# Two groups of set-up work placed later in a transformer block written in float32: row statistics of eight input tiles, and the loads for the next weight fold

## The chip, the cores and the metric

The kernel runs on one core of a Trainium2 chip. The metric is device time in microseconds (us). Three runs of the kernel before gave a median of 1911.75 us (1910.15 to 1915.11).

## The reference, cut to what matters

One block of a transformer on x of 2048 rows by 1024 columns, all float32:

```python
qkv = layernorm(x) @ wqkv                      # 32 heads of 32
pq, pk = q @ w_phi, k @ w_phi                  # per head
phi = concat(softmax(p), softmax(-p))          # for pq and for pk
o = (phi_q @ (phi_k.T @ v)) / (phi_q @ sum(phi_k) + 1e-6)
h = x + o @ wo
out = h + relu(layernorm(h) @ w1) @ w2
```

The layer norm divides by the square root of variance plus 1e-5 and has no learned scale.

## The kernel before, in words

**Tiles.** x is cut into 16 row tiles of 128 rows (t = 0 to 15). Products are float32 made of three matmuls each: every operand is split into a high part and a low part, and `mm3` (lines 181 to 184) adds high by high, high by low and low by high in PSUM. The second of the three, line 183, is the first that reads the low part of a weight.

**Items and steps.** The work of TensorE is a list of items, and each item has steps. In the stage of this change an item is one row tile times a set s of 512 weight columns: eight steps k = 0 to 7, one for each 128 rows of the weight, each step three matmuls. Items 0 to 31 (steps 0 to 255) are the keys and values of x tiles 0 to 7: eight items for each s = 0 to 3, so that s = 1 starts at step 64, s = 2 at step 128 and s = 3 at step 192. Items 32 to 47 (from step 256) are the queries of the same tiles, then the keys, values and queries of x tiles 8 to 15 follow.

**An order written out by hand.** Nothing is scheduled by a compiler. `when(step, f, ...)` puts a call beside a step, and the program walks through the steps in order and lets each call issue its instructions. Each engine, and the queue of SP that starts almost all DMAs, then works through its own instructions strictly in that order. An instruction that waits holds all that stand behind it on its engine. A step number says only where in these queues an instruction stands, not when it runs. Inside one step the calls run in the order in which they were registered in the code.

**What stands around the change in the queues.**

- Weight units. For each (s, k) SP loads a 128 by 512 tile `raw` (lines 324 and 325, or 328 for queries; six buffers), ScalarE copies the high part into `w` (line 125), and VectorE (odd units) or GpSimd (even units) subtracts to get the low part (line 129). There are ten buffers for `w`. Eight hold the present s, so the units k = 0 and 1 of the next s are made ahead, and each later one only when the last item of the present s has used up a unit.
- Folds. w_phi is multiplied into the weights of keys and queries once. Fold p (p = 1 to 7) stands at the steps `FOLD_STEPS` = 31, 64, 104, 144, 176, 206, 232. There TensorE multiplies two loaded tiles `wt` (`fold_all`, line 290) and VectorE transposes the result (`fold_turn`, line 300). Six steps later SP stores 1 MB to DRAM (`fold_store`, line 311), and 17 steps later the raw loads that read it may be issued. `wt_load` (line 274) issues the two loads of 512 KB for the next fold; it has four buffers.
- Sums of w1 and w2. From step 24 on, every ten steps, number n: `t_load` at step 24 + 10n (`b`, 512 KB, line 351), four subtractions in place on GpSimd at 31 to 34 + 10n (`t_sum`, line 361), `t_store` at 37 + 10n (line 364). `b` has two buffers, so load n waits on the SP queue until store n - 2 has landed.
- Statistics of x tiles 8 to 15. These tiles are loaded twice. The first time, with key ("s", t), only the two numbers of the layer norm are taken: `ln_load` at step `early` = 80 + 16 (t - 8) (`xin`, 512 KB, two buffers, line 215), `ln_stats` on VectorE at `early` + 10 (two statistics instructions of line 221 and one of line 223, result `mv`), `ln_power` on GpSimd at `early` + 13 (lines 230 to 232, three instructions on one column, result `scx`). The second load, from step 241 on, reads the rows again and normalizes them with `scx`.
- Keys and values of an item n, after its matmuls: VectorE (lines 428 to 432), ScalarE exponential at 8n + 11 (line 436), VectorE at 8n + 13 (lines 441 to 444, result `kphi`), GpSimd's running sum `zacc` at 8n + 18 (line 452), and small matmuls that read `kphi` (line 463).

Of the kernel before, what the change touches and what calls it, by code (L numbers as in the profile page):

```python
# [140 lines left out]
def kernel(  # L141
# [12 lines left out]
    v, act, pool, pe, sp = nc.vector, nc.scalar, nc.gpsimd, nc.tensor, nc.sync  # L154
# [34 lines left out]
    def do(n, k, f, *args):  # L189
        at[n, k].append((f, args))  # L190
# [17 lines left out]
    xin, xst, xnt = {}, {}, {}  # L208
# [644 lines left out]
    def item(gen, *args, keys):  # L853
        items.append((gen, args + (keys,)))
        steps.extend((k,) for k in keys)
        return len(items) - 1
# [11 lines left out]
    for b, tiles in enumerate(groups):  # L868
        for hf in range(2):

            pairs = b == 0 and hf == 0
            for j in range(0, 4, 2 if pairs else 1):
# [3 lines left out]
                for half in range(2):  # L876
                    n = item(wo_pair, tiles[j:j + 2], hf, half, keys=[("wo", hf, 4 * half + k // 2) for k in range(8)])
# [18 lines left out]
    def x_part(t):  # L896
        return [x[t * P:(t + 1) * P, :]]
# [6 lines left out]
    def when(step, f, *args):  # L904

        if step < 8 * first_up:
            do(step // 8, step % 8, f, *args)
        else:
            do(first_up + (step - 8 * first_up) // 4, step % 4, f, *args)
# [4 lines left out]
    for t in range(1, NT):  # L914
        n = t - 1 if t < HT else q_n[1, t - HT] + 1
        turn = 8 * n + 1
        if t < HT:
            stages = X_STEPS.get(t, (turn - 22, turn - 12, turn - 9, turn - 6, turn, turn + 3))
        else:

            early = 80 + 16 * (t - HT)
            when(early, ln_load, ("s", t), x_part(t))
            when(early + 10, ln_stats, ("s", t))
            when(early + 10, xin.pop, ("s", t))
            when(early + 13, ln_power, ("s", t))
            load_ = turn - 88 + 8 * (t - HT) if t < HT + 4 else turn - 36
            stages = (load_, None, None, turn - 8, turn, turn + 3)
        for step, f, *args in zip(stages, (ln_load, ln_stats, ln_power, ln_norm), [("x", t)] * 4):
            if step is not None:
                when(step, f, *args, *([x_part(t)] if f is ln_load else []))  # L930
        do(n, 0, x_open, t)
        for j in range(2):
            when(stages[4 + j], ln_turn, ("x", t), j, lambda t=t: xT[t])
# [6 lines left out]
    for p, n in enumerate(FOLD_STEPS, 1):  # L940
        when(n, fold_all, p)
        when(n, fold_turn, p)
        when(n + 6, fold_store, p)
        when(n + 17, fold_ready, p)
        if p < 7:
            when(n + 2, wt_load, p + 1, sp)


    for (hf, s, t), n in kv_n.items():
# [146 lines left out]
    for b in range(2):  # L1096
        for m in DOWN:
            n = down_n[b, m, NP - 1] + 1
# [112 lines left out]
```

## Time and profile before

| | |
|---|---|
| median of three runs | 1911.75 us |
| profiled execution, its own time | 1911.77 us |
| its span, first to last instruction | 1910.0 us |
| TensorE busy with matmuls | 1884.6 us (99%) |
| VectorE, ScalarE, GpSimd busy | 1045.3, 739.2, 975.8 us |
| mean granted TensorE clock | 0.996 |
| mean DMA rate | 226 GB/s |

How to read it: the profile comes from one execution. Its time is 1.8 us over its span and agrees with the median of the runs. A stage is read from its own part of the trace: the times below are microseconds from the start of the span. In the timeline of an engine each row has the start, the duration, the engine (SPq is the queue of SP), the line, the instruction with what it writes and reads, how many are merged, and in brackets how long the engine sat idle before it and for whom. A wait for several things is put down to the one that came last.

### The profile page before, as it was taken

The numbers are of one execution on the slowest core, as the hardware profiler recorded it, in microseconds if no ns is written. First come the engines' busy times: TensorE is split into PE (matmuls) and PEld (weight loads), VectorE is DVE, ScalarE is ACT, GpSimd is POOL, SyncE is SP. The second block draws the span as 40 slices with busy tenths as digits, with TensorE's granted clock in tenths as the row PEclk, the third lists the DMA queues.
The fourth block names the chain that finished last, engine by engine and source line by source line (L and its number), as shares of the span: only waits on it lengthen the run. The fifth ranks groups of instructions, "written<-read, shape, count | busy, mean of one in ns | idle before, by whom it ended". The sixth has DMA issues, their size and how long they took to land.

```text
span 1910.0 us, 31857 instructions
## 1 busy us (share of the span) xinstructions
PE 1884.6 (99%) x11640; PEld 1540.9 (81%) x11640; DVE 1045.3 (55%) x1685; ACT 739.2 (39%) x1258; POOL 975.8 (51%) x961
## 2 busy tenths in 40 slices
PE   9979999999999999999999999999999999999999
PEld 7757778877878888888888888888888888888887
DVE  7858668767669866545644564344433333343333
ACT  5322225322222212345454464444444444444442
POOL 4667751789955988523333232222244444444443
PEclk9989999999999999999999999999999999999999
DMA  6879785666666667696777897566677677877775
GB/s 213 264 232 303 250 268 189 220 189 210 206 192 204 210 207 242 216 302 219 254 257 231 262 290 235 178 189 194 213 243 225 191 240 225 250 214 218 216 215 178
DMA packets 292366, 432.17 MB, mean 226 GB/s; under 512 B 24049, under 2 KB 150001, under 8 KB 292209
## 3 DMA queue, kind: packets, MB, share of 16 engines
q1 hardware_dynamic: 275312, 413.36, 68.5%
q10 hardware_dynamic: 16896, 16.78, 2.6%
q8 instruction: 91, 1.49, 0.3%
q14 instruction: 67, 0.54, 0.1%
HBM read 292.68 MB, written 137.36 MB: 225 GB/s over the span
## 4 chain that ended last, share of the span: by engine, by line
PE 83%; POOL 7%; DMA 6%; issue 1%; DVE 1%; SPq 0%; ACT 0%; POOLq 0%; DVEq 0%; ACTq 0%
PE mm L182 21%; PE mm L183 21%; PE mm L184 21%; PE ac L183 4%; PE ac L184 4%; PE ac L182 4%; POOL b L361 3%; DMA b<-in_w_dram 3%; PE tp L183 2%; PE tp L184 2%; PE tp L182 2%; POOL w L129 2%; DMA t<-b 2%; DMA xin<-in_x_dram 1%; PE tp L245 1%
## 5 line engine op out<-in xcount | busy, mean ns | idle before, releaser
L129 POOL TENSOR_TENSOR w<-raw,w 128x512 fp32r<-128x512 f32 x355 | 474.7, 1339 | 717.7 <-ACT w L125 665.0
L125 ACT ACTIVATE w<-raw 128x512 fp32r<-128x512 f32 x686 | 408.7, 626 | 507.8 <-PE mm L184 246.6
L129 DVE TENSOR_TENSOR w<-raw,w 128x512 fp32r<-128x512 f32 x331 | 270.5, 818 | 529.1 <-ACT w L125 525.8
L183 PE MATMUL mm<-w,xT 128*128 128x512 f32 x768 | 302.8, 394 | 14.7 <-POOL w L129 14.2
L182 PE MATMUL mm<-w,xT 128*128 128x512 f32 x768 | 309.3, 403 | 0.0
L184 PE MATMUL mm<-w,xT 128*128 128x512 f32 x768 | 301.2, 392 | 0.0
L182 PE MATMUL mm<-hT,w 128*128 128x512 f32 x672 | 262.7, 391 | 0.0
L183 PE MATMUL mm<-hT,w 128*128 128x512 f32 x672 | 261.6, 389 | 0.6 <-DVE hT L753 0.6
L184 PE MATMUL mm<-hT,w 128*128 128x512 f32 x672 | 261.6, 389 | 0.0
L361 POOL TENSOR_TENSOR b<-b 128x256 f32<-128x256 f32 x224 | 181.5, 810 | 99.2 <-DMA b<-in_w_dram 84.5
L183 PEld LDWEIGHTS mm<-w,xT 128*128 128x128 f32 x768 | 145.3, 189 | 48.9 <-POOL w L129 19.1
L182 PEld LDWEIGHTS mm<-w,xT 128*128 128x128 f32 x768 | 145.2, 189 | 35.1 <-issue 4.2
L184 PEld LDWEIGHTS mm<-w,xT 128*128 128x128 f32 x768 | 145.2, 189 | 30.7
L182 PE MATMUL mm<-w 128*128 128x512 f32 x392 | 152.5, 389 | 0.0
L183 PE MATMUL mm<-w 128*128 128x512 f32 x392 | 152.5, 389 | 0.0
L184 PE MATMUL mm<-w 128*128 128x512 f32 x392 | 152.5, 389 | 0.0
L183 PEld LDWEIGHTS mm<-hT,w 128*128 128x128 f32 x672 | 126.2, 188 | 26.8 <-DVE hT L753 1.1
L184 PEld LDWEIGHTS mm<-hT,w 128*128 128x128 f32 x672 | 126.1, 188 | 26.4
L182 PEld LDWEIGHTS mm<-hT,w 128*128 128x128 f32 x672 | 126.1, 188 | 26.0 <-ACT c L776 0.3
L436 ACT ACTIVATE ke<-ke 128x512 f32<-128x512 f32 x64 | 40.4, 631 | 121.2 <-DVE ke L432 121.2
L182 PEld LDWEIGHTS mm<-w 128*128 128x128 f32 x392 | 73.6, 188 | 15.3
L183 PEld LDWEIGHTS mm<-w 128*128 128x128 f32 x392 | 73.6, 188 | 15.3
(169 smaller groups left out, 3135.1 us busy)
## 6 DMA issues: line engine op xcount, KB each, us to landing
raw<-t SPq DMA_DIRECT2D x224, 256.0 KB, 3.9
raw<-ad SPq DMA_DIRECT2D x196, 256.0 KB, 3.0
raw<-in_w_dram SPq DMA_DIRECT2D x168, 256.0 KB, 3.1
b<-in_w_dram SPq DMA_DIRECT2D x56, 512.0 KB, 3.9
t<-b SPq DMA_DIRECT2D x56, 512.0 KB, 4.7
ad<-c SPq DMA_DIRECT2D x112, 256.0 KB, 3.5
ad<-s SPq DMA_DIRECT2D x84, 256.0 KB, 4.2
ed<-qe ACTq DMA_DIRECT2D x32, 512.0 KB, 4.4
```

Source lines behind the costliest of these rows:

```text
L125: nc.scalar.activation(w[:, 0, :], raw[1], AF.Copy)
L129: eng.tensor_tensor(out=w[:, 1, :], in0=raw[1], in1=w[:, 0, :].bitcast(F32), op=ALU.subtract)
L182: pe.matmul(ps, a_hi, b_hi, start=first, stop=False, skip_group_check=more)
L183: pe.matmul(ps, a_hi, b_lo, start=False, stop=False, skip_group_check=more)
L184: pe.matmul(ps, a_lo, b_hi, start=False, stop=last, skip_group_check=more)
L245: pe.transpose(pt[:, k, :], xn[:, (4 * j + k) * P:(4 * j + k + 1) * P], ident)
L361: pool.tensor_tensor(out=tsum[j, *out], in0=tsum[j, *a], in1=tsum[j, *b], op=ALU.subtract)
L436: act.activation(e_of[key], e_of[key], AF.Exp)
```

## The change

For x tiles 8 to 15, `ln_stats` goes from `early` + 10 to `early` + 18, and `ln_power` from `early` + 13 to `early` + 22. The loads `ln_load` stay at `early`. The bookkeeping call `xin.pop` goes along and issues nothing. Apart from that, `wt_load` for fold p + 1 goes from two steps behind fold p to twelve: from steps 33, 66, 106, 146, 178, 208 to 43, 76, 116, 156, 188, 218. No instruction is added or removed.

```diff
             early = 80 + 16 * (t - HT)
             when(early, ln_load, ("s", t), x_part(t))
-            when(early + 10, ln_stats, ("s", t))
-            when(early + 10, xin.pop, ("s", t))
-            when(early + 13, ln_power, ("s", t))
+            when(early + 18, ln_stats, ("s", t))
+            when(early + 18, xin.pop, ("s", t))
+            when(early + 22, ln_power, ("s", t))
...
         when(n + 6, fold_store, p)
         when(n + 17, fold_ready, p)
         if p < 7:
-            when(n + 2, wt_load, p + 1, sp)
+            when(n + 12, wt_load, p + 1, sp)
```

## The prediction

> **What bounds the kernel now.** I read the page first. TensorE is busy almost the whole span, so a change of order can win only what TensorE loses: idle time and time at a low clock.
>
> ```profile
> PE 1884.6 (99%) x11640; PEld 1540.9 (81%) x11640; DVE 1045.3 (55%) x1685; ACT 739.2 (39%) x1258; POOL 975.8 (51%) x961
> PEclk9989999999999999999999999999999999999999
> ```
>
> The only lowered clock digit is the third slice of 47.75 us (95 to 143 us), which is where the moved calls stand. The waits of TensorE from 100 to 140 us, and its timeline there:
>
> ```profile
> PE mm L183 <- POOL w L129: 9.6, 2, 8.4
> ```
>
> ```profile
> 118.78 0.43 PE L463 MATMUL ac<-kphi,vt 128*32 128x64 f32 x16 [0.67 <-DVE kphi L444]
> ...
> 122.91 0.50 PE L183 MATMUL mm<-w,xT 128*128 128x512 f32 x1 [1.21 <-POOL w L129]
> ...
> 132.93 0.80 PE L183 MATMUL mm<-w,xT 128*128 128x512 f32 x1 [8.37 <-POOL w L129]
> ...
> 138.40 0.43 PE L183 MATMUL mm<-w,xT 128*128 128x512 f32 x1
> 138.66 0.39 PE L184 MATMUL mm<-w,xT 128*128 128x512 f32 x1
> 138.89 0.39 PE L182 MATMUL mm<-w,xT 128*128 128x512 f32 x1
> ```
>
> TensorE stops where set s = 2 begins (step 128): at the low part of unit k = 2, and for 8.37 us at that of k = 4. Behind the stop the clock is low: from 132.93 to 138.40 stand 12 intervals, 5.47 us, which at the later pace of 0.23 us take 2.7. The whole place costs 0.67 + 1.21 + 8.37 + 2.74 = **13.0 us**. That is the ceiling of the gain here.
>
> Next question: why are the low parts late? GpSimd and VectorE around it:
>
> ```profile
> 101.11 0.22 POOL L230 TENSOR_SCALAR scx<-mv 128x1 f32<-128x1 f32 x1
> ...
> 102.30 1.57 POOL L361 TENSOR_TENSOR b<-b 128x256 f32<-128x256 f32 x2
> 103.83 1.29 POOL L129 TENSOR_TENSOR w<-raw,w 128x512 fp32r<-128x512 f32 x1
> ...
> 113.18 0.22 POOL L230 TENSOR_SCALAR scx<-mv 128x1 f32<-128x1 f32 x1 [2.41 <-DVE mv L223]
> ...
> 116.53 2.70 POOL L361 TENSOR_TENSOR b<-b 128x256 f32<-128x256 f32 x3 [1.68 <-DMA b<-in_w_dram]
> ...
> 121.60 1.26 POOL L129 TENSOR_TENSOR w<-raw,w 128x512 fp32r<-128x512 f32 x1
> 127.75 1.12 POOL L361 TENSOR_TENSOR b<-b 128x256 f32<-128x256 f32 x1 [4.89 <-DVE mv L223]
> ...
> 131.17 1.71 POOL L129 TENSOR_TENSOR w<-raw,w 128x512 fp32r<-128x512 f32 x1
> ...
> 134.34 1.28 POOL L129 TENSOR_TENSOR w<-raw,w 128x512 fp32r<-128x512 f32 x1
> ```
>
> ```profile
> 111.56 1.29 DVE L221 BATCH_NORM_STATS2 st<-xin 128x6 f32<-128x512 f32 x2 [6.90 <-DMA xin<-in_x_dram]
> ...
> 126.18 1.29 DVE L221 BATCH_NORM_STATS2 st<-xin 128x6 f32<-128x512 f32 x2 [5.15 <-DMA xin<-in_x_dram]
> ```
>
> The low part of k = 4 (131.17, ending at 132.88) stands behind sums of w1 and w2 that begin at 127.75. The trace puts their wait down to `mv` of VectorE. It can't be that: `t_sum` reads only `b`, and the three instructions that read this `mv` come after 134.34. What landed at the same moment is the load of `b`, issued at 122.22 (SP's rows below) and 5.4 us under way:
>
> ```profile
> DMA to landing us min/median/max: 5.4/5.4/5.4
> ```
>
> So the large wait is one for SP and the DMAs, and the visible waits of VectorE for `xin` (6.90 and 5.15 us) are mostly not its cause. SP's rows:
>
> ```profile
> 74.66 0.93 SPq L274 DMA_DIRECT2D wt<-in_wqkT_dram  x2
> 75.71 0.52 SPq L364 DMA_DIRECT2D t<-b  x1
> ...
> 84.30 0.38 SPq L351 DMA_DIRECT2D b<-in_w_dram  x1
> 84.80 0.52 SPq L364 DMA_DIRECT2D t<-b  x1
> ...
> 93.56 0.43 SPq L351 DMA_DIRECT2D b<-in_w_dram  x1
> ...
> 105.15 0.34 SPq L324 DMA_DIRECT2D raw<-wpk  x1
> ...
> 106.54 0.53 SPq L364 DMA_DIRECT2D t<-b  x1
> ...
> 112.91 0.38 SPq L351 DMA_DIRECT2D b<-in_w_dram  x1
> 113.39 0.93 SPq L274 DMA_DIRECT2D wt<-in_wqkT_dram  x2
> 114.41 0.53 SPq L364 DMA_DIRECT2D t<-b  x1
> ...
> 122.22 0.38 SPq L351 DMA_DIRECT2D b<-in_w_dram  x1
> ```
>
> A load of `b` can go only when the store before last has landed. The stores of 75.71 and 114.41 each have 1 MB of `wt` right in front of them and hold the next load until 84.30 and 122.22, 8.6 and 7.8 us later. The store of 106.54, without `wt`, takes 6.4, and that of 84.80 takes 4.9:
>
> ```profile
> DMA to landing us min/median/max: 4.9/4.9/4.9
> ```
>
> So a loop of load, sums, store runs from DMA to GpSimd and back through SP, and the units for TensorE stand in the same queues.
>
> **The change, part by part.** Nothing is removed or added; I follow the loop through the new order, from its own rows.
>
> *wt for fold 3, step 66 to 76.* The store of 75.71 loses the 1 MB in front of it. It lands after 4.9 instead of 8.6, at 80.6, and the load of 84.30 goes 3.7 us earlier. But `wt` now stands behind that load and before the store of 84.80, which then takes 7.8 instead of 4.9. That store waits for sums too; I let it go 1.5 earlier, and it lands at 83.3 + 7.8 = 91.1. The load of 93.56 goes 2.4 us earlier; a third of the shift is given back.
>
> *Power of tile 8, step 93 to 102.* Its three instructions run from 101.11 to 102.30 between sums, ahead of the low part at 103.83 that frees a raw buffer. SP waits for that buffer at 105.15, and the store of 106.54 stands behind. Taking 1.2 us away there brings this store 2.4 + 1.2 = 3.6 us forward, to 102.9, and the load of 112.91 to 109.3. Behind the low part the same three cost their 1.2 us again, covered by the wait for the next `b`.
>
> *wt for fold 4, step 106 to 116.* The store of 114.41 can go at 109.8. Without `wt` it lands at 114.7 by the 4.9 above. The load of 122.22 goes at 114.8, 7.4 us earlier, and lands with its 5.4 at 120.2. From 127.75 to the end of the low part of k = 4 GpSimd took 5.1 us, so that ends at 125.3.
>
> *Statistics and power of tile 9, steps 106 to 114 and 109 to 118.* VectorE no longer stands before `kphi` for 6.90 us, so TensorE's 0.67 us goes. GpSimd's wait of 2.41 us at 113.18 goes; the three instructions now stand just ahead of the low part of k = 2, which by the shifted sums ends near 120, before TensorE needs it at 121. So 1.21 goes too. Bounds for this term: 0 left, or 2.3 if the load of 112.91 comes no earlier.
>
> *What is late next.* Without the two small waits TensorE asks for k = 4 at 132.93 - 8.37 - 1.9 = 122.7 and gets it at 125.3: **2.6 us** wait. The next even unit takes GpSimd 2.7 us more (132.88 to 135.62), TensorE's two units only 6 x 0.227 = 1.4: another **1.4**. Bounds: 0 if `b` lands 4 us earlier still, 9.6 if nothing moves.
>
> *The clock.* Does a wait of 2.6 us still lower it? The nearest row is another short wait:
>
> ```profile
> 530.15 0.50 PE L183 MATMUL mm<-w,xT 128*128 128x512 f32 x1 [1.40 <-POOL w L129]
> ...
> 530.96 0.59 PE L183 MATMUL mm<-w,xT 128*128 128x512 f32 x1
> ```
>
> 0.8 us after a wait of 1.40 us the matmuls slow down. I take one such stretch of 3.4 us at half pace: **1.7 us**, between 0 and the 2.7 of now. [...]
>
> *Folds 5, 6 and 7.* Their `wt` also goes ten steps later. For folds 5 and 6, 20 and 18 steps of 0.68 us are left, 12 to 14 us, for a landing of 8.3 us at most (row below): nothing, unless SP lags by more than 4. Fold 7 has 14 steps, 9.5 us, and is close:
>
> ```profile
> 202.66 0.84 SPq L274 DMA_DIRECT2D wt<-in_wqkT_dram  x2
> ...
> 207.36 0.53 SPq L364 DMA_DIRECT2D t<-b  x1
> ```
>
> ```profile
> L290 PE MATMUL tp<-wt,wphi x32: 374/374/398, 213.9 to 214.9; 32*32 32x256 f32 x32
> ```
>
> ```profile
> DMA to landing us min/median/max: 3.8/6.4/8.3
> ```
>
> Its load moves behind the store of 207.36 and lands 3.8 to 8.3 us later, 211.7 to 216.2, against a fold at 213.9. If SP comes forward as far as TensorE, that is a wait of 0 to 2.3 us; the median 6.4 gives 214.3: 0.4. Where the queries begin, TensorE waits too:
>
> ```profile
> 239.63 0.50 PE L183 MATMUL mm<-w,xT 128*128 128x512 f32 x1 [1.40 <-POOL w L129]
> ```
>
> If the loop comes forward less than TensorE, this wait grows by the difference, 0 to 3 us. Together I take **0.6**, near the low end, since loop (7.4) and TensorE (13.0 - 2.6 - 1.4 - 1.7 = 7.3) come forward about alike.
>
> **Sum**, against the profiled execution's own 1911.77 (span 1910.0 and 1.8 around it; the median of the runs is 1911.75, the same): 13.0 - 2.6 - 1.4 - 1.7 - 0.6 = 6.7 us less, **1905.1 us**. About 0.3% (5.7 us: below 1906.0 or above 1917.5) is what a measurement of this kernel can tell from no change.
>
> **The rivals.**
>
> *The wait goes wholly.* If the load of 122.22 comes 11 us earlier instead of 7.4, all 13.0 go: 1898.8. For it: the queues couple, and each early store makes the next earlier. Against it: `b` would have to land at 116. Chance 0.10.
>
> *The clock stays up.* [...] Chance 0.12.
>
> *The same bytes, elsewhere.* `wt` still passes through the same queue, only one `b` later. If the give-back eats all of the shift, as it ate a third of the first, the 8.37 stays almost whole and only 0.67 and 1.21 go: 1910. Against it: at the second fold the give-back falls on a load that k = 4 doesn't wait for. Chance 0.13.
>
> *Fold 7 waits for its weights (slower).* TensorE can't pass the matmuls of line 290. It turns the change into a loss once `wt` lands so late that the wait passes what was won before. `wt` stands behind the store of 207.36, which waits for sums; if these slip by 5 us as the early ones did, and the landing takes 8.3, it lands at 221, 7 us after 213.9. With the clock (2.7) that is 10 us against 0 to 6 won: 1912 to 1922, say 1917. For it: here the rows leave no slack. Against it: SP's lag there was small, and the load of 202.66 landed fast. Chance 0.20.
>
> **How the numbers follow.** Forecast 0.45 (1902 to 1909, two thirds of it below 1906.0), wholly gone 0.10, clock up 0.12, same bytes 0.13, fold 7 0.20. Faster by over 0.3%: 0.30 + 0.10 + 0.12 = 0.52. Slower: 0.14 of the last rival. Within: 0.15 + 0.13 + 0.06 = 0.34. The range runs from 1899 (all gone) to 1914, and leaves out the worst half of the last rival and a little below. The forecast's own range is 1902 to 1909.
>
> **What would show it.** In the profile after: the stores that stood behind `wt` at 75.71 and 114.41 land in 5 to 6.5 us; the load of `b` that precedes unit k = 4 goes about 7 us earlier against the matmuls; TensorE's wait there is 2 to 4 us; VectorE no longer waits for `xin`; line 290 shows no wait over 2 us. Wrong would be an unchanged wait of 8 us without any wait of VectorE for `xin` (then my loop isn't what bounds it), a wait of TensorE for `wt`, or new waits at steps 192 and 256 as large as what was won.

## The result, and the profile after

| | before | changed |
|---|---|---|
| median, 6 runs each | 1912.72 us | 1904.09 us (1903.57 to 1908.77) |
| ratio to before | 1 | 0.9959, 95% interval 0.9944 to 0.9973 |
| the same again, 7 runs against 11 | 1912.25 us | 1905.85 us; 0.9967, 0.9954 to 0.9980 |
| profiled execution | 1911.77 us | 1908.77 us; second time 1903.10 us |

The change makes the kernel 6 to 9 us faster; 1905.1 was forecast. The first profiled execution of the changed kernel is the slowest of its six, 3.0 us under that of before. What it shows is read with that in mind.

The page of the changed kernel has no lowered clock digit any more:

```profile
PEclk9999999999999999999999999999999999999999
```

The waits of TensorE in total (in all, times, longest), from the answer on waits:

```profile
PE mm L183 <- POOL w L129: 8.7, 10, 2.6
...
PE tp L290 <- DMA wt<-in_wqkT_dram: 2.8, 2, 1.9
```

The low parts cost 8.7 us instead of 14.2, and a wait is there that the kernel before didn't have: for the weights of a fold. TensorE's timeline has each wait with its place:

```profile
122.32 0.50 PE L183 MATMUL mm<-w,xT 128*128 128x512 f32 x1 [1.21 <-POOL w L129]
...
126.61 0.50 PE L183 MATMUL mm<-w,xT 128*128 128x512 f32 x1 [2.63 <-POOL w L129]
...
129.34 0.80 PE L183 MATMUL mm<-w,xT 128*128 128x512 f32 x1 [0.34 <-POOL w L129]
...
208.91 0.45 PE L290 MATMUL tp<-wt,wphi 32*32 32x256 f32 x8 [0.89 <-DMA wt<-in_wqkT_dram]
...
211.61 0.45 PE L290 MATMUL tp<-wt,wphi 32*32 32x256 f32 x8 [1.86 <-DMA wt<-in_wqkT_dram]
```

The 8.37 us at unit k = 4 are 2.63 us. SP's queue shows why; the rows stand in the new order:

```profile
75.10 0.53 SPq L364 DMA_DIRECT2D t<-b  x1
...
78.41 0.37 SPq L351 DMA_DIRECT2D b<-in_w_dram  x1
78.82 2.27 SPq L274 DMA_DIRECT2D wt<-in_wqkT_dram  x2
81.21 0.53 SPq L364 DMA_DIRECT2D t<-b  x1
...
109.50 0.38 SPq L351 DMA_DIRECT2D b<-in_w_dram  x1
109.98 0.52 SPq L364 DMA_DIRECT2D t<-b  x1
...
115.34 0.37 SPq L351 DMA_DIRECT2D b<-in_w_dram  x1
115.76 1.40 SPq L274 DMA_DIRECT2D wt<-in_wqkT_dram  x2
```

The two stores that had `wt` in front of them now hold the next load of `b` for 3.3 us (75.10 to 78.41) and 5.4 us (109.98 to 115.34), not 8.6 and 7.8. The load ahead of unit k = 4 goes at 115.34 instead of 122.22. GpSimd behind it:

```profile
114.06 2.71 POOL L361 TENSOR_TENSOR b<-b 128x256 f32<-128x256 f32 x3 [4.04 <-DMA b<-in_w_dram]
...
119.26 0.22 POOL L230 TENSOR_SCALAR scx<-mv 128x1 f32<-128x1 f32 x1
...
121.00 1.27 POOL L129 TENSOR_TENSOR w<-raw,w 128x512 fp32r<-128x512 f32 x1
122.22 0.74 POOL L361 TENSOR_TENSOR b<-b 128x256 f32<-128x256 f32 x1
...
124.85 1.71 POOL L129 TENSOR_TENSOR w<-raw,w 128x512 fp32r<-128x512 f32 x1
```

Here the sums of 122.22 no longer wait for `b`: they follow the low part of k = 2 without a gap. The power of tile 9 stands directly ahead of that low part and takes from 119.26 to 121.0. The sums in front of both begin at 114.06; before, they began at 116.53.

### The profile page after: what moved, and what is told of

Read it like the earlier page. It is cut to its first block, busy times and chain, and to the rows that moved or that the text cites. A ratio compares the mean times of both kernels' runs of the same rounds, so it can differ in the third digit from the quotient of the medians.

```text
span 1907.0 us, 31851 instructions
## 1 busy us (share of the span) xinstructions
PE 1882.6 (99%) x11640; PEld 1539.3 (81%) x11640; DVE 1048.1 (55%) x1685; ACT 740.3 (39%) x1258; POOL 974.6 (51%) x961
## 4 chain that ended last, share of the span: by engine, by line
PE 79%; POOL 12%; DMA 6%; issue 2%; DVE 1%; SPq 1%; ACT 0%; POOLq 0%; ACTq 0%; DVEq 0%
PE mm L182 19%; PE mm L183 19%; PE mm L184 19%; PE ac L183 4%; PE ac L182 4%; PE ac L184 4%; POOL b L361 3%; PE tp L183 2%; PE tp L184 2%; PE tp L182 2%; DMA b<-in_w_dram 2%; POOL w L129 2%; POOL ez L574 2%; DMA t<-b 1%; PE tp L245 1%
## 5 line engine op out<-in xcount | busy, mean ns | idle before, releaser
L182 PEld LDWEIGHTS mm<-w 128*128 128x128 f32 x392 | 73.6, 188 | 15.3
L184 PEld LDWEIGHTS mm<-w 128*128 128x128 f32 x392 | 73.6, 188 | 15.3
L183 PEld LDWEIGHTS mm<-w 128*128 128x128 f32 x392 | 73.6, 188 | 15.3
```

Of the source, the lines that this page charges most:

```text
L182: pe.matmul(ps, a_hi, b_hi, start=first, stop=False, skip_group_check=more)
L183: pe.matmul(ps, a_hi, b_lo, start=False, stop=False, skip_group_check=more)
L184: pe.matmul(ps, a_lo, b_hi, start=False, stop=last, skip_group_check=more)
```

## The experiments

Each was timed against the kernel before on its chip. Two theories were on trial at first. Mine: a loop of load, sums and store for w1 and w2 runs behind TensorE, and the order matters by what it puts into the loop's way. The rival: VectorE waits for `xin`, and everything stands behind it.

### Statistics and power alone

```diff
-            when(early + 10, ln_stats, ("s", t))
+            when(early + 18, ln_stats, ("s", t))
...
-            when(early + 13, ln_power, ("s", t))
+            when(early + 22, ln_power, ("s", t))
```

> Only the statistics and the power go later; the loads for the folds stay two steps behind their fold. Loop theory (the load of b that stands ahead of unit k = 4 waits for a store behind 1 MB of wt): the two small waits of TensorE go (0.67 and 1.21 us), the load of b comes only 1 to 2 us earlier, the wait at unit k = 4 stays at 6 to 8 us with its three low-clock windows; 2 to 4 us less than the kernel before, ratio about 0.998 to 0.999. Rival (VectorE waiting for xin holds everything): VectorE's wait was the cause, so the 8.37 us fall to about the 2.6 us of the changed kernel, and since no fold waits for its weights it is even faster than the changed kernel, ratio 0.993 to 0.995.

Measured: 0.9988 (0.9980 to 0.9997). TensorE's timeline of this kernel:

```profile
123.19 0.50 PE L183 MATMUL mm<-w,xT 128*128 128x512 f32 x1 [2.33 <-POOL w L129]
...
130.11 0.79 PE L183 MATMUL mm<-w,xT 128*128 128x512 f32 x1 [5.26 <-POOL w L129]
```

VectorE's waits for `xin` between 60 and 220 us fell from 17.4 us to 2.0, and still 7.6 of the 10.3 us of waiting are left for TensorE at step 128. So VectorE's wait for `xin` wasn't the main cause. The load of `b` ahead of k = 4 went at 120.18, 2.0 us earlier, as expected. The wait for k = 4 fell below my 6 to 8, with less half clock behind it than the 10.24 us of the kernel before, three times 3.41 (mean granted clock of the execution 0.998, there 0.996), and that for k = 2 grew instead of going.

### The loads for the folds alone

```diff
-            when(n + 2, wt_load, p + 1, sp)
+            when(n + 12, wt_load, p + 1, sp)
```

> Only the loads for the folds go ten steps later; statistics and power stay. Loop theory: most of the shift of the load of b remains (5 to 6 of 7 us), TensorE's wait at unit k = 4 falls to 3 to 5 us although VectorE still waits for xin there, and folds 6 and 7 wait for their weights as in the changed kernel (2 to 3 us): 2 to 5 us less than before, ratio 0.997 to 0.999. Rival (VectorE waiting for xin): the 8.37 us stay and the waits at the folds come on top, so 2 to 5 us more than before, ratio 1.001 to 1.003.

Measured: 0.9987 (0.9978 to 0.9995), inside my range. TensorE waits 4.61 us for k = 4 while VectorE still waits 12.7 us for `xin` between 60 and 220 us. The load of `b` ahead of k = 4 went at 118.39, 3.8 us earlier and not 5 to 6. Fold 7 waits twice; fold 6, where I expected a wait too, doesn't:

```profile
129.73 0.79 PE L183 MATMUL mm<-w,xT 128*128 128x512 f32 x1 [4.61 <-POOL w L129]
...
211.88 0.45 PE L290 MATMUL tp<-wt,wphi 32*32 32x256 f32 x8 [1.36 <-DMA wt<-in_wqkT_dram]
...
214.06 0.68 PE L290 MATMUL tp<-wt,wphi 32*32 32x256 f32 x8 [1.35 <-DMA wt<-in_wqkT_dram]
```

### The load for fold 7 early again, and those for folds 5 to 7

```diff
-            when(n + 12, wt_load, p + 1, sp)
+            when(n + (12 if p < 6 else 2), wt_load, p + 1, sp)
```

and with `p < 4` for the second.

> The changed kernel with the load for fold 7 back at two steps behind fold 6. If the wait of TensorE for wt at fold 7 is a real cost: that wait (1.9 us) and the low-clock window behind it (1.7 us) go, the trace ends 2 to 4 us before that of the changed kernel, ratio to before 0.993 to 0.995. Rival (paid again where the queries begin): the wait for the low parts at the start of the queries grows by as much, and the time is that of the changed kernel, ratio 0.996.

> The changed kernel with the loads for folds 5, 6 and 7 back at two steps behind the fold before; those for folds 2, 3 and 4 stay late. Loop theory: the gain at step 128 needs only the loads for folds 3 and 4, so TensorE's wait at unit k = 4 stays near 2.6 us, no fold waits for its weights, and the trace ends 3 to 5 us before that of the changed kernel, ratio to before 0.992 to 0.995. Rival (paid again): the loop falls back behind the earlier loads, new waits for low parts come at steps 192 or 256, ratio 0.996 or above.

Measured: 0.9966 (0.9953 to 0.9978) and 0.9965 (0.9953 to 0.9977). Both rivals were right in time: the waits for `wt` go, and nothing is won. New waits stand at the next place where a set of units begins. With fold 7 early, the start of the queries waits 2.33 us in all, where the changed kernel waited 0.73:

```profile
235.49 0.65 PE L183 MATMUL mm<-w,xT 128*128 128x512 f32 x1 [1.91 <-POOL w L129]
...
237.41 0.80 PE L183 MATMUL mm<-w,xT 128*128 128x512 f32 x1 [0.42 <-POOL w L129]
```

With folds 5 to 7 early it is set s = 3, where the changed kernel waited 0.78 us; half clock follows from 180.97 to 187.80, 6.83 us (mean granted clock of this execution 0.998):

```profile
179.70 0.50 PE L183 MATMUL mm<-w,xT 128*128 128x512 f32 x1 [2.32 <-POOL w L129]
...
182.17 0.80 PE L183 MATMUL mm<-w,xT 128*128 128x512 f32 x1 [0.60 <-POOL w L129]
```

The second trace shows the payment more cleanly than the first: with folds 5 to 7 early TensorE is at fold 4 when the changed kernel is, with fold 7 early it is 2.8 us later there, although the order up to that place is the same. The times point to a limit that lies elsewhere. The runs with a slower loop, further down, loosen it.

### Power alone, and the change without the statistics

The first is the kernel before with only `ln_power` at `early` + 22, run twice. The second is the changed kernel with the statistics back:

```diff
-            when(early + 18, ln_stats, ("s", t))
+            when(early + 10, ln_stats, ("s", t))
```

> Only the power on GpSimd goes from early + 13 to early + 22; the statistics and the loads for the folds stay. If what matters in the first half of the change is that GpSimd doesn't stop for the statistics ahead of the sums and low parts: the same as with statistics and power moved, ratio about 0.999, the wait at unit k = 4 near 5 us, although VectorE still waits 5 to 7 us for xin. Rival (the place of the statistics on VectorE matters): as the kernel before, ratio 1.000, with the 8.37 us still there.

> The kernel of the power alone once more, on one chip with the next two: 0.997 at its first time against 0.999 for statistics and power together. If the place of the statistics on VectorE is worth nothing either way, power alone and statistics with power have one ratio, 0.997 to 0.999. Rival (the later statistics cost something): power alone stays faster than both by 0.001 or more, near 0.997.

> The changed kernel with the statistics back at early + 10; power and the loads for the folds stay late. If the statistics' place is worth nothing: the time of the changed kernel, ratio 0.995 to 0.997, the wait at unit k = 4 near 2.6 us, with VectorE waiting for xin again. Rival (VectorE's wait holds the copies and low parts): 2 us or more slower than the changed kernel, ratio 0.997 or above.

Measured: power alone 0.9972 (0.9959 to 0.9985) and then 0.9987 (0.9977 to 0.9996); power with the loads, without the statistics, 0.9966 (0.9954 to 0.9978). The first of the two runs of power alone had looked better than statistics with power (0.9988); the second is the same. My 5 us for the wait at k = 4 were wrong, it stayed at 7.40 us, and at 7.58 in the second run, with 2.25 and 2.63 at k = 2:

```profile
123.22 0.50 PE L183 MATMUL mm<-w,xT 128*128 128x512 f32 x1 [2.25 <-POOL w L129]
...
132.27 0.80 PE L183 MATMUL mm<-w,xT 128*128 128x512 f32 x1 [7.40 <-POOL w L129]
```

The traces show hardly any gain at that place, the times a small one; that is left open. The second kernel has the time of the changed one (0.9967 at its second measurement) with VectorE still waiting for `xin` (9.6 us between 60 and 220 us), and at unit k = 4, where I expected about 2.6 us:

```profile
126.64 0.50 PE L183 MATMUL mm<-w,xT 128*128 128x512 f32 x1 [3.50 <-POOL w L129]
```

So no worth of the statistics' place could be measured in time. In the traces TensorE waits 7.6 us at step 128 with statistics and power, and 9.7 and 10.2 us with power alone, so the place may be worth something there; these are single executions.

### A slower loop, without and with the change

The sums of w1 and w2 come every 11, then every 12 steps instead of every 10, as far as number 25. The later ones keep their ten steps and begin at 350: numbers 26 and 27, at steps 284 and 294 before, go to 350 and 360, and the rest, from step 368 on before, follow from 370. The work is the same.

```diff
-        step = 24 + 10 * n
-        if step > 8 * q_n[1, 0] - 20:
-            step += 64
+        step = 24 + 11 * n if n < 26 else 350 + 10 * (n - 26)
```

> The kernel before, with the sums of w1 and w2 every 11 steps instead of every 10 as far as number 25, and from step 350 every 10 as it was (the same work, all of it before step 664). If the loop of load, sums and store is what runs behind TensorE and holds the queues of SP and GpSimd: the wait at unit k = 4 falls from 8.37 us to below 3 us without any of the edits of the change, the waits at the start of the queries go, ratio 0.993 to 0.996. Rival (the place of wt, statistics and power is the cause in itself): the 8.37 us stay within 2 us, ratio 0.998 to 1.001.

> The changed kernel with the same slower pace of the sums. If what the change wins at step 128 is partly given back because the loop limits the whole stretch up to step 320: with the slower loop nothing is given back, the waits at steps 128, 192, 256 and for the wt of fold 7 all fall below 1.5 us, and it is 4 to 8 us faster than the changed kernel, ratio to before 0.991 to 0.994. Rival (given back for another reason, GpSimd's own work): the time of the changed kernel, ratio 0.995 to 0.997.

> The changed kernel with the sums every 12 steps as far as number 25, then every 10 from step 350. If the loop still limits at 11 steps, another 1 to 3 us go, ratio 0.992 to 0.994. Rival (at 11 steps the loop keeps up): the time of the kernel at 11 steps, ratio 0.994, or a little more because the last loads come closer to those of x tiles 8 to 15.

> The kernel before with the sums every 12 steps as far as number 25 and every 10 from step 350. If the loop is the root and the change only trims it: with a loop that has slack the change is worth little, so this one is within 0.001 of the changed kernel at 12 steps (0.993), ratio 0.992 to 0.995. Rival (the change is worth as much beside a slow loop): ratio 0.996 to 0.998.

> The changed kernel once more, to place it against its variants (folds 5 to 7 early 0.9965, fold 7 early 0.9966, statistics back 0.9966). If the waits at the folds are only paid again elsewhere when they are avoided, and the statistics' place is worth nothing, all of these are one time: ratio 0.996 to 0.997. Rival (the change as a whole is better than each variant): 0.995 to 0.996 again.

| kernel | median | ratio to before |
|---|---|---|
| before, 11 steps | 1901.69 us | 0.9948 (0.9929 to 0.9966) |
| changed, 11 steps | 1900.12 us | 0.9940 (0.9922 to 0.9959) |
| changed, 12 steps | 1899.73 us | 0.9931 (0.9919 to 0.9944) |
| before, 12 steps | 1897.24 us | 0.9928 (0.9914 to 0.9941) |
| changed, again | 1905.85 us | 0.9967 (0.9954 to 0.9980) |

One number in the kernel before wins more than the change. At 11 steps, with statistics, power and `wt` at their old places, the wait for k = 4 is that of the changed kernel:

```profile
126.27 0.62 PE L183 MATMUL mm<-w,xT 128*128 128x512 f32 x1 [2.62 <-POOL w L129]
```

At 11 steps the sums around step 128 stand at 119 to 122 and at 130 to 133, with 10 steps at 121 to 124 and at 131 to 134; they have hardly moved against that place. At 12 steps the wait for k = 4 is 0.83 us, although VectorE still waits 9.3 us for `xin` between 60 and 220 us:

```profile
123.81 0.50 PE L183 MATMUL mm<-w,xT 128*128 128x512 f32 x1 [0.83 <-POOL w L129]
...
125.59 0.50 PE L183 MATMUL mm<-w,xT 128*128 128x512 f32 x1 [0.81 <-DVE w L129]
...
128.41 0.50 PE L183 MATMUL mm<-w,xT 128*128 128x512 f32 x1 [1.16 <-DVE w L129]
```

```profile
122.57 1.29 DVE L221 BATCH_NORM_STATS2 st<-xin 128x6 f32<-128x512 f32 x2 [5.59 <-DMA xin<-in_x_dram]
...
124.02 1.52 DVE L129 TENSOR_TENSOR w<-raw,w 128x512 fp32r<-128x512 f32 x1
```

TensorE's waits at step 128 come to 3.2 us here, with no half clock behind them (its matmuls stay 0.23 us apart). Of these 2.0 us are for low parts of VectorE, which stand right behind its wait for `xin`. So that wait does cost something once the loop is out of the way, but little.

SP's own waits between 40 and 300 us show what went, from the queue's answer on waits of the kernel before, the changed one, the changed one at 11 and the one before at 12 steps (loads of `b` waiting for a store to land: us in all, times, longest; the one before at 11 steps has 63.5 us):

```profile
SPq L351 <- DMA t<-b: 83.2, 20, 8.2
```

```profile
SPq L351 <- DMA t<-b: 67.5, 19, 5.9
```

```profile
SPq L351 <- DMA t<-b: 48.7, 17, 6.2
```

```profile
SPq L351 <- DMA t<-b: 48.7, 15, 7.8
```

At 12 steps the kernels with and without the change have one time within their intervals: beside a loop with slack, the new order is worth nothing that these runs can measure. Whether the loop still limits at 11 steps isn't settled, since the intervals of 11 and 12 steps overlap. The changed kernel measured again has the ratio of its three variants (0.9965, 0.9966, 0.9966), as the loop would have it. The changed kernel at 11 steps won 4 to 6 us over itself at 10, and its waits at steps 128, 192 and 256 are each below 0.8 us, as expected. But nearly all of its time was won at 11 steps without the change: the two differ by 1.6 us.

One thing these runs don't separate: a slower pace also leaves GpSimd fewer sums per step. GpSimd had room all the same. Between 60 and 240 us it was busy 132.5 us in the kernel before and 129.8 at 12 steps, and it waited for `b` 36.5 us (with the 4.89 that the trace puts down to `mv`) and 34.6. What shrank is SP's wait for the stores.

When TensorE came to three places, in us, in one profiled execution of each kernel (first matmul of fold 4, step 144, and of fold 7, step 232; the transposes of line 482 at step 533):

| kernel | fold 4 | fold 7 | line 482 |
|---|---|---|---|
| before | 145.2 | 213.9 | 443.0 |
| statistics and power | 142.4 | 213.5 | 442.8 |
| power alone, two executions | 143.7, 145.6 | 213.5, 215.3 | 442.1, 442.7 |
| loads for the folds | 141.8 | 211.9 | 442.8 |
| power and loads | 140.0 | 209.0 | 435.5 |
| changed | 138.2 | 208.9 | 439.8 |
| changed, second execution | 137.7 | 208.3 | 435.6 |
| changed, fold 7 early | 141.0 | 210.8 | 440.6 |
| changed, folds 5 to 7 early | 138.2 | 213.2 | 439.9 |
| before, 11 steps | 137.5 | 206.9 | 433.8 |
| before, 12 steps | 136.0 | 204.7 | 430.0 |
| changed, 11 steps | 132.7 | 202.2 | 429.0 |
| changed, 12 steps | 134.8 | 203.5 | 430.5 |

Up to fold 4 the order is the same in the changed kernel and in the two with early folds. Four executions of it stand at 137.7 to 141.0 us, so single executions differ by up to 3.3 us there. Each half of the change wins about 3 us at fold 4 and has lost nearly all of it at line 482, but with one execution each that is hardly more than this spread. The whole change wins 4.2 to 7.5 us at fold 4; in its own two executions it wins 7.0 and 7.5 and keeps 3.2 and 7.4.

## Why the prediction held, point by point

- **What bounds the stage: right.** The wait was put to the loop, against the trace's own entry (`mv`). The kernel at 12 steps shows it: the wait for k = 4 nearly goes while VectorE still waits for `xin`.
- **The stores and the load: right at the end of the chain, not at each step.** The load ahead of k = 4 was to go at 114.8 and went at 115.34; the low part was to be ready at 125.3 and was at 126.56 (124.85 + 1.71). On the way the load of 93.56 went 0.9 us earlier, not 2.4, and the store of 106.54 2.4, not 3.6. This store then held the next load 5.4 us instead of 6.4, which wasn't forecast, and so the load of 112.91 came to 109.50, where 109.3 was said.
- **Waits of TensorE at step 128: right in the sum, not in each.** 0.67 went, as said. The 1.21 at k = 2 was to go and stayed 1.21: the sums ahead of it began 2.5 us earlier, not 3.6, as `b` was issued 3.4 us earlier and took 4.4 us to land instead of 3.5, and the power of tile 9 took 1.7 us, not the 1.2 that I gave it. k = 4 was 2.6 and is 2.63, since TensorE asked for it and got it both 1.3 us later than worked out; the next was 1.4 and is 0.34. At fold 4 TensorE is 7.0 us earlier, 7.3 were worked out.
- **The clock: right.** Behind step 128 there is one stretch at half clock in both profiled executions. In the first it lasts 3.41 us (127.3 to 130.7), which costs 1.7 us; in the second the matmuls are 0.43 us apart from 126.55 on and 0.23 again from 129.92. The rival that it stays up was wrong here. No run shows a length of waiting up to which nothing is lost in clock: 2.63 us were followed by half clock in the first execution, and after 2.63 us at unit k = 2 in the second run of power alone the matmuls kept their 0.23 us.
- **Folds and queries, 0.6 us: mis-sized in one execution.** In the first profiled execution fold 7 waits 0.89 + 1.86 = 2.75 us, its loads having landed in 5.7 and 7.6 us where 6.4 was taken, and the clock is at half once more from 212.6 to 216.0, 3.41 us, which costs 1.7 us. With s = 3 (0.78) and the queries (0.73 for 2.05) that is 3.9 us. In the second execution fold 7 waits 1.44 without the low clock, and the same sum is 0.7. A wait of TensorE for `wt` had been named as a sign of being wrong, and it came. The rival of fold 7 had the right place and too high a price.
- **What the sum left out** is that the waits behind step 128 aren't separate. Taken away at fold 7, they seem to come back at the queries; taken away at folds 5 to 7, they come back at s = 3. What TensorE wins early it keeps only as far as the loop follows.
- **The total: partly luck.** 6.7 us were forecast, 8.6 and 6.4 measured, and the two profiled executions end 3.0 and 8.7 us before that of the kernel before. Of these, 1.7 us are the half clock at 531.0 in the kernel before, which neither has and which the forecast doesn't hold.
- **The same bytes, elsewhere:** in the one trace of each half of the change alone the late stretch takes nearly everything back; of the whole it isn't true.

Open: why each half keeps 0.1% in time but nearly nothing by line 482 in its trace, and why the two executions of the changed kernel differ by 5.7 us in span. For the first, the profiled execution of the loads for the folds is the slowest of its eleven (1912.91 us, median 1911.00), which is a part of it. For the second, they differ in the waits at fold 7 and in one low-clock stretch, 3.0 us together.

## What to carry to other kernels

When one wait in a long queue goes and another of about its size comes, look for the loop that feeds both, and test it by giving the loop slack before its neighbours are rearranged: here one pace, 12 steps for 10, won 15 us in the kernel before, and the new order 6 to 9. Don't trust the releaser of a row where the waiting instruction reads nothing of it; look for the transfer that landed at the same moment. Waits behind one limit can't be summed: take each away alone and see whether the end moves.

## What the runs showed of the hardware

In the traces' records of the granted clock, half clock stands from 128.2 to 138.4 us (10.24 us) and from 531.0 to 534.4 (3.41 us) in the kernel before, and from 127.3 to 130.7 and 212.6 to 216.0 (3.41 us each) in the first profiled execution of the changed one. Each of the four begins during or less than 1.1 us after a wait of TensorE: 8.37 us up to 132.93, 1.40 us up to 530.15, 2.63 us up to 126.61, and 1.86 us up to 211.61. In these stretches the matmuls of 128x512 are 0.43 us apart, outside them 0.23.

The length of the last wait alone doesn't tell in these runs whether half clock follows. It followed 1.40 us at 530.15, but not 0.65 and 1.40 us at 237 to 240 in the same execution, nor 1.40 us at 522.82 in the second execution of the changed kernel. It followed 2.63 us in the first execution of the changed kernel; in the second run of power alone, 2.63 us up to 123.75 were followed by matmuls 0.23 us apart until the next wait, from 125.4 on. What decides isn't settled by these runs.
